# A re-ordered attention and gated-MLP kernel: K copied whole, batch 1's output turned by DMA, the flag read in mid-stream, the last two output tiles apart

## The chip, the cores and the metric

The kernel runs on one core of a Trainium2 chip. The core has five engines that work through their own queues in order and meet by semaphores: TensorE (PE; its weight loads are shown apart as PEld), VectorE (DVE), ScalarE (ACT), GpSimd (POOL) and SyncE (SP). POOL and SP also issue DMAs. The metric is the device time of one execution in microseconds; the time before is the median of three runs, 164.16 us (163.69 to 164.3).

## What is computed

Shapes: 4 batches, 8 heads, 768 positions, head width 64, 8 blocks of 96 positions.

```python
P = sort_net                                  # [B, H, 8, 8]
for _ in range(5):                            # exp, rows to sum 1, columns to sum 1
    P = exp(P - max(P)); P = P / sum(P, -1); P = P / sum(P, -2)
k_s, v_s = P mixed into the blocks of k, v    # einsum 'bhij,bhjcd->bhicd'
attn = softmax(q_block @ k_s_block.T / 8)     # within each block
x = (attn @ v_s) with heads side by side      # [B, 768, 512]
h = relu(x @ w_in); u, v = halves of h        # 512 columns each
v_n = (v - mean(v)) / sqrt(var(v) + 1e-6)
v_s = w_spatial @ v_n + b_spatial             # over the positions
out = (u * v_s) @ w_out                       # [B, 768, 512]
```

## The kernel before

The whole work is cut into small units, and the string ORDER (lines 18 to 48) lists them by hand: each item is a unit's name and its arguments, and the unit's instructions are put into the queues of their engines in this order. There is no scheduler behind it: an engine takes its own instructions in the order of the list, and waits are added where a tile is written, read or used again. PSUM has four tiles of two banks, ps0 to ps3; most units name the one that they write, so a unit also waits until the last reader of that tile is done. Letters A, D and P name the engine that copies a result out (ACT, DVE, POOL).

The units, with their lines (b a batch, hp a pair of heads, ih a half of the blocks):

- S0 loads sort_net; SK:n (line 223) is one round of the normalisation: an exp on ACT, then sums, reciprocals and products on DVE. MA (204) and MC (210) make a mask sum and a spread identity on DVE.
- L:x:b (156) issues a load on POOL's queue; BI (187) loads the bias b_bc on SP's queue. The input tiles come from a pool of 8, so later loads wait for the units that read the first ones. Each of the 8 semaphores of a queue is used in turn, so a DMA also waits for the one eight before it.
- DM (216) is six dummy matmuls on PE. PR, P0, PC, PD make the mixing matrices (PD on POOL, two parts a batch).
- QT and QQ (312, 318) turn q on PE, for one pair of heads and for two. KT (361, copies at 292 to 297) mixes and turns k. With two letters (DA, AD) its result is copied in two halves by two engines.
- VT and VB (batch 0), VM and VC (batches 1 to 3) bring the mixed v into block order; VC (400) does it by eight DMAs on SP's queue, four in each item.
- SC (413) is the scores of a pair of heads and a half, with the exp on ACT (427); AT (459) is attention times v, with a reciprocal and a product on DVE (475, 476) into x_sb.
- x_sb must be turned into xT. XT (491) does it on PE, eight transposes of 96 columns and one copy; XD (482) does a whole half by one DMA transpose on SP's queue (486). In the kernel before, batches 0 and 1 use XT, batches 2 and 3 XD.
- VP (507) and UP (549) are the two halves of x @ w_in with relu; ST, LN, LA (525 to 547) are the normalisation of v; WT (501) turns w_spatial; SP (564; a unit, not the engine of that name) is the spatial product with the bias added on DVE (575); GT (581) is the gate's product, on DVE or POOL; OP (588), OE (602) and OS (608) are the product with w_out, its copy from PSUM and its store on SP's queue.
- CK (617), CF (632) and LF (638): two checks on the sums make one flag, which every engine loads into a register; if it is set, a slower general path runs behind the main one.

The main path ends in this order:

```python
SP:3:3:0 GT:P:3:2 SP:0:3:1 OP:2:2:4 GT:D:3:1 OS:2:0 OS:2:2 OE:A:2:4 GT:D:3:0 SP:3:3:3 OP:1:3:0:0:3 GT:D:3:3
OP:0:3:4:0:3 OP:-1:3:0:3:4 OE:A:3:0:1:2 OP:3:3:2:0:3 CK OS:2:4 OP:-1:3:2:3:4 OE:D:3:2:1:2 OE:A:3:0:0:1 OP:-1:3:4:3:4
OS:3:0:1:2 OS:3:0:0:1 OE:A:3:2:0:1 OS:3:2:0:1 OS:3:2:1:2 OE:A:3:4:0:1 OS:3:4:0:1 OE:A:3:4:1:2 OS:3:4:1:2 CF:2 LF
```

OP:1:3:0:0:3 is the first three of four row blocks of tiles 0 and 1 of batch 3 in ps1, OP:-1:3:0:3:4 the fourth, which needs the last gate product. OE and OS then work on one tile of the pair.

Of the kernel before, what the change touches and what calls it, by code (L numbers as in the profile page):

```python
# [8 lines left out]
FP32 = mybir.dt.float32  # L9
# [39 lines left out]


# [12 lines left out]
def kernel(  # L63
# [19 lines left out]
    BH = B * H  # L83
    DM = H * D
# [3 lines left out]
    FC = DH // 128  # L88
# [9 lines left out]
    moe = ctx.enter_context(tc.tile_pool(name="moe", bufs=2))  # L98
# [3 lines left out]
    def ps_tile(n, dt=FP32):  # L102
        return psum.tile([128, 2, 512 if dt == FP32 else 1024], dt, name=f"ps{n}", tag=f"ps{n}")

    def copy(eng, out, in_):
        if eng == "A":
            nc.scalar.copy(out=out, in_=in_)  # L107
        else:
            nc.vector.tensor_copy(out=out, in_=in_)
# [29 lines left out]
    w_out_sb = const.tile([128, FC, DM], BF16, name="w_out_sb")  # L139
# [8 lines left out]
    st = {}  # L148
# [465 lines left out]

    def u_CK():
        nc.vector.memset(bad, 0.0)
        over = lambda col, rows, in_, op, bound, test: (
            nc.vector.tensor_reduce(out=ends[0:rows, col:col + 1], in_=in_, axis=AX.X, op=op),  # L620
            nc.vector.tensor_scalar(
                out=bad[0:rows, col:col + 1], in0=ends[0:rows, col:col + 1],
                scalar1=bound, scalar2=None, op0=test),
        )
# [103 lines left out]
```

## Time and profile before

| | |
|---|---|
| time, median of 3 runs | 164.16 us (163.69 to 164.3) |
| the profiled execution's own time | 163.99 us |
| its span, from the first instruction to the last | 162.2 us |
| PE busy | 147.9 us, 91% |
| DVE, ACT, POOL busy | 117.7, 84.3, 33.7 us |
| DMA | 23.2 MB, mean 143 GB/s |
| granted TensorE clock, mean | 0.988 |

The profile shows one execution. Busy is the time in which an engine has an instruction in work; PE's matmuls overlap, so that its busy time says only where it does not stand still. The chain of waits follows back from the last instruction what each step waited for; PE has 78% of it here, ACT 7%, DVE 6%. The costliest group is the spatial product (line 569, 192 matmuls, 33.2 us). DMA landings are counted from the issue to the last byte's semaphore.

### The profile page before, as it was taken

How to read it: one execution, taken by the hardware profiler on the slowest of the kernel's cores; microseconds unless marked ns; L12 is line 12 of the kernel's file. 1: busy time of each engine (PE TensorE's matmuls, PEld its weight loads, DVE VectorE, ACT ScalarE, POOL GpSimd, SP SyncE). 2: the span in 40 equal slices, each digit the busy share in tenths (PEclk: the TensorE clock that was granted, in tenths of full speed). 3: DMA queues.
4: the chain of work that ended last, by engine and by line, in shares of the span. 5: the costliest groups of instructions: out<-in, count | busy, mean ns of one | idle time of the engine just before them, and what ended most of it. 6: DMA issues, size and time to landing. Idle time of an engine off the chain costs nothing.

```text
span 162.2 us, 3967 instructions
## 1 busy us (share of the span) xinstructions
PE 147.9 (91%) x1646; PEld 89.5 (55%) x1657; DVE 117.7 (73%) x265; ACT 84.3 (52%) x118; POOL 33.7 (21%) x39
## 2 busy tenths in 40 slices
PE   6988999899999979999999999999999999999700
PEld 2345777756677755455657656555666445655300
DVE  4797899667897853748898888789787798267500
ACT  3144999858976476577654453557400155402420
POOL 7946322470000434280000001600000000120000
PEclk9999999999999999999999999999999999999995
DMA  2999999999999990479985996002059200243370
GB/s 12 191 204 205 203 205 205 210 220 237 271 206 204 206 172 0 69 133 148 184 188 94 225 149 195 0 36 97 0 107 237 113 0 0 91 172 129 129 250 25
DMA packets 27351, 23.20 MB, mean 143 GB/s; under 512 B 7232, under 2 KB 24128, under 8 KB 27328
## 3 DMA queue, kind: packets, MB, share of 16 engines
q0 software_dynamic: 14864, 12.19, 48.5%
q1 hardware_dynamic: 12464, 10.70, 25.8%
q8 instruction: 14, 0.23, 0.5%
q14 instruction: 9, 0.07, 0.1%
HBM read 24.78 MB, written 6.29 MB: 192 GB/s over the span
## 4 chain that ended last, share of the span: by engine, by line
PE 78%; ACT 7%; DVE 6%; DMA 2%; issue 2%; DVEq 0%; ACTq 0%
PE ps L569 20%; PE ps L557 13%; PE ps L514 13%; PE ps L595 11%; PE ps L468 4%; PE ps L422 4%; PE ps L363 3%; PE ps L390 3%; PE ps L307 3%; ACT ex L427 2%; ACT kt L107 2%; PE ps L498 2%; DMA out_dram<-o_sb 1%; PE ps L504 1%; ACT o_sb L107 1%
## 5 line engine op out<-in xcount | busy, mean ns | idle before, releaser
L569 PE MATMUL ps<-wspT,v_sb 128*128 128x384 bf16 x192 | 33.2, 326 | 0.0
L427 ACT ACTIVATE ex<-ps 96x768 bf16<-96x768 f32 x32 | 24.4, 806 | 12.4 <-PE ps L422 12.3
L585 POOL TENSOR_TENSOR gt<-z,u_sb 128x768 bf16<-128x768 f32 x7 | 11.4, 1640 | 92.7 <-DVE z L575 42.1
L569 PEld LDWEIGHTS <-v_sb 128*128 128x128 bf16 x192 | 18.2, 98 | 11.9 <-issue 0.2
L575 DVE TENSOR_TENSOR z<-ps,b_bc 128x768 f32<-128x768 f32 x16 | 15.3, 957 | 11.6 <-PE ps L569 11.5
L557 PE MATMUL ps<-xT,w_in_sb 128*128 128x384 bf16 x128 | 23.3, 326 | 0.0
L476 DVE TENSOR_TENSOR x_sb<-ps,rec_all 96x512 bf16<-96x512 f32 x32 | 22.0, 687 | 1.1
L514 PE MATMUL ps<-w_in_sb,xT 128*128 128x512 bf16 x89 | 22.2, 379 | 0.4
L595 PE MATMUL ps<-w_out_sb,gt 128*128 128x512 bf16 x93 | 22.0, 379 | 0.2
L107 ACT COPY o_sb<-ps 128x1024 f32<-128x1024 f32 (+1 forms) x12 | 9.8, 835 | 14.8 <-PE ps L595 12.9
L531 DVE BATCH_NORM_STATS2 stats<-v_sb 128x6 f32<-128x512 bf16 x24 | 16.2, 677 | 1.0 <-ACT v_sb L113 0.9
L113 ACT ACTIVATE v_sb<-ps 128x1024 bf16<-128x1024 f32 (+1 forms) x8 | 7.4, 920 | 17.6 <-PE ps L514 17.6
L557 PEld LDWEIGHTS <-w_in_sb 128*128 128x128 bf16 x128 | 11.8, 98 | 7.6
L595 PEld LDWEIGHTS <-gt 128*128 128x128 bf16 x96 | 9.2, 98 | 10.2
L514 PEld LDWEIGHTS <-xT 128*128 128x128 bf16 x96 | 9.0, 98 | 9.6 <-DVE x_sb L476 0.2
L113 ACT ACTIVATE u_sb<-ps 128x768 bf16<-128x768 f32 x13 | 10.6, 812 | 5.1 <-PE ps L557 5.0
L107 ACT CAST kt<-ps 128x768 bf16<-128x768 f32 (+1 forms) x14 | 8.7, 641 | 7.9 <-PE ps L363 5.5
L468 PEld LDWEIGHTS <-ex 96*128 96x128 bf16 x256 | 10.5, 97 | 3.6 <-issue 0.3
L468 PE MATMUL ps<-vb,ex 96*128 96x65 bf16 x256 | 11.9, 193 | 0.1
L219 PE MATMUL ps<-warm 128*128 128x512 bf16 x35 | 9.9, 436 | 1.3 <-DVE warm L192 1.3
L422 PE MATMUL ps<-qT,kt 64*128 64x96 bf16 x256 | 9.5, 204 | 1.6 <-ACT kt L107 1.3
L422 PEld LDWEIGHTS <-kt 64*128 64x128 bf16 x256 | 6.2, 94 | 6.9 <-issue 3.8
(87 smaller groups left out, 179.0 us busy)
## 6 DMA issues: line engine op xcount, KB each, us to landing
out_dram<-o_sb SPq DMA_DIRECT2D x9, 512.0 KB, 4.3
q_in<-in_q_dram POOLq DMA_DIRECT2D x4, 768.0 KB, 18.0
k_in<-in_k_dram POOLq DMA_DIRECT2D x4, 768.0 KB, 15.1
v_in<-in_v_dram POOLq DMA_DIRECT2D x4, 768.0 KB, 21.5
vb<-vm SPq DMA_DIRECT2D x24, 99.0 KB, 3.1
out_dram<-o_sb SPq DMA_DIRECT2D x6, 256.0 KB, 3.2
ws_in<-in_moe_w_spatial_dram POOLq DMA_DIRECT2D x2, 576.0 KB, 26.4
w_in_sb<-in_moe_w_in_dram POOLq DMA_DIRECT2D x2, 512.0 KB, 26.0
```

The costliest lines, as they stand in the source:

```text
L107: nc.scalar.copy(out=out, in_=in_)
L113: nc.scalar.activation(out=out, in_=in_, func=AF.Relu)
L422: nc.tensor.matmul(t[:, hh, 0:HW].rearrange("p (g x) -> p g x", g=G)[:, :, ii * TB:(ii + 1) * TB], lhsT=kT[rows, i * BLK:i * BLK + 128], r ...
L427: nc.scalar.activation(out=e_tile(b, hp, ih).rearrange("p h (x g) -> p h x g", g=G), in_=t[0:BLK, :, 0:HW].rearrange("p h (g x) -> p h x g ...
L468: nc.tensor.matmul(t[:, hh, ii * VW:ii * VW + D + 1], lhsT=e[:, c:c + 128], rhs=vb[b % 2][:, ih * NI + ii, 2 * hp + hh, 0:D + 1], start=Tr ...
L476: nc.vector.tensor_mul(out=x_sb[:, hp].rearrange("p i (h d) -> p h i d", h=2), in0=tv[:, :, :, 0:D], in1=_raw_ap(rec, 0, [rec.ap[0], [NI, ...
L514: nc.tensor.matmul(t[:, x, :], lhsT=st["xT", b][:, n // 3, kc, (n % 3) * 128:(n % 3 + 1) * 128], rhs=w_in_sb[:, kc, DH:DFF], start=(kc == ...
L531: nc.vector.bn_stats(out=stats, in_=st["v_sb", b, n])
L557: nc.tensor.matmul(t[:, x, 0:HW], lhsT=w_in_sb[:, kc, mc * 128:(mc + 1) * 128], rhs=st["xT", b][:, ih, kc, :], start=(kc == 0), stop=(kc = ...
L569: nc.tensor.matmul(t[:, x, 0:HW], lhsT=st["v_sb", b, n][:, mc * 128:(mc + 1) * 128], rhs=wspT[:, 3 * x:3 * x + 3, n, :], start=(n == 0), s ...
L575: nc.vector.tensor_add(out=z.rearrange("p (x c) -> p x c", x=2), in0=t[:, :, 0:HW], in1=b_bc.rearrange("p (x c) -> p x c", x=2),)
L595: nc.tensor.matmul(t[:, x, :], lhsT=st["gt", b, mc][:, (n0 + x) * 128:(n0 + x + 1) * 128], rhs=w_out_sb[:, mc, :], start=(mc == 0), stop=( ...
```

## The change

ORDER is written anew, and three units are added for the last two output tiles. What differs in it:

- Every KT copies its result whole, by one engine (eight on ACT, eight on DVE). Before, seven of 16 were copied in two halves.
- Batch 1's x is turned by two DMA transposes (XD:1:0, XD:1:1) instead of four XT units; batch 0 keeps its four XT.
- BI, the load of the bias, stands at the start instead of in batch 1's scores. The loads come in another order: q of batch 1 ahead of v and k, v of batch 2 ahead of its q and k, w_out behind k of batch 3, and q of batch 3 earlier.
- The order of heads, halves and units and the engine of many copies differ: five of the six W copies are on DVE instead of three, ten of the 16 gate products on POOL instead of seven, two of the 13 relus of VP less on DVE.
- CK and CF stand ahead of the last six SP units and LF ahead of the last four; before, LF stood behind the last store. The branch stays at the end.
- Tiles 4 and 5 of batch 3 are computed, copied and stored one by one (OH, OI, OJ), in PSUM tiles and output tiles of their own; the output tiles come from the pool of z.
- All six DM units are there in both.

```diff
--- before.py
+++ after.py
@@ -16,35 +16,35 @@
 
 
 ORDER = """
-S0 CO SK:0 L:q:0:0:8 L:k:0:0:8 L:v:0:0:8 L:v:1:0:8 BH SK:1 SK:2 L:k:1:0:8 ID IV:2 MC IV:0 DM:1:6:512 L:q:1:0:8 SK:3
-L:wv MA DM:3:6:512 DM:1:6:512 DM:2:6:512 SK:4 L:wsb QT:1:A:0:0 MB QT:0:D:0:1 QT:3:A:0:2 DM:2:6:512 PR:3 DM:2:6:512
-P0:0:2 KT:1:A:0:0 P0:6:8 L:wu P0:4:6 PC:D P0:2:4 PD:1:0:4 QT:0:D:0:3 L:wsa IV:1 PD:1:4:8 KT:2:DA:0:1 KT:3:DA:0:3
-SC:1:0:0:0 SC:0:0:1:1 KT:2:D:0:2 SC:3:0:0:1 L:q:2:0:8 VT:1:D:0:0 SC:0:0:2:0 L:k:2:0:8 VT:2:D:0:1 SC:3:0:3:1 VB:1:D:0:0
-VT:0:A:0:2 VB:2:D:0:1 VT:3:A:0:3 AT:1:0:0:1 VB:0:A:0:2 L:v:2:0:8 AT:2:0:0:0 L:wo VB:3:D:0:3 PD:3:0:4 SC:1:0:3:0
-AT:0:0:1:1 SC:2:0:1:0 SC:3:0:2:1 AT:1:0:3:1 VM:2:A:1:0 AT:0:0:1:0 VM:3:A:1:1 AT:1:0:2:1 VM:2:A:1:2 XT:0:D:0:1:0
-KT:3:A:1:2 AT:1:0:2:0 KT:0:A:1:0 AT:2:0:3:0 XT:3:A:0:1:2 KT:0:A:1:3 QQ:1:D:1:0 VM:2:A:1:3 XT:0:D:0:0:2 XT:3:D:0:0:0
-SC:1:1:0:0 QQ:2:D:1:2 VC:1:0:4 KT:0:A:1:1 VP:1:D:0:0:1 SC:3:1:2:1 ST:0:0 SC:0:1:3:1 VP:2:A:0:4:5 WT:3:A:5 WT:1:D:4
-VP:0:A:0:3 ST:0:5 PD:2:0:4 SC:2:1:1:0 ST:0:3 SC:1:1:2:0 UP:3:A:0:1:0 VP:2:A:0:2 VC:1:4:8 ST:0:1 ST:0:4 AT:0:1:0:0
-ST:0:2 WT:1:A:3 SC:3:1:3:0 LN:0:0:6 UP:2:A:0:0:1 AT:0:1:2:0 AT:1:1:3:0 LA:0:0 PD:2:4:8 UP:3:A:0:1:1 WT:0:D:0 LA:0:2
-LA:0:1 LA:0:4 AT:2:1:2:1 LA:0:3 XT:1:A:1:0:2 LA:0:5 L:v:3:0:8 WT:3:A:1 UP:0:A:0:0:0 WT:3:D:2 BI SC:1:1:0:1 QQ:2:A:2:2
-AT:3:1:1:0 AT:0:1:3:1 SP:1:0:3 SC:2:1:1:1 XT:0:D:1:1:2 XT:3:A:1:0:0 AT:1:1:0:1 AT:2:1:1:1 SP:0:0:2 XT:2:A:1:1:0
-GT:P:0:3 KT:1:AD:2:3 KT:3:AD:2:2 KT:0:DA:2:0 KT:2:A:2:1 GT:P:0:2 QQ:1:A:2:0 SC:0:2:3:0 VM:3:D:2:3 SP:2:0:1 VM:1:A:2:2
-VM:0:A:2:1 VP:3:D:1:0:1 VM:2:A:2:0 SP:1:0:0 SC:0:2:2:1 SC:2:2:1:1 GT:P:0:1 VC:2:4:8 VC:2:0:4 ST:1:1 VP:3:A:1:4:5
-SC:1:2:1:0 SC:0:2:3:1 GT:P:0:0 UP:2:A:1:0:0 PD:3:4:8 ST:1:0 ST:1:4 VP:3:D:1:2:3 VM:2:A:3:3 VM:1:A:3:0 OP:0:0:2 ST:1:2
-OE:A:0:2 L:k:3:0:8 AT:1:2:3:1 VM:2:A:3:2 UP:3:A:1:1:0 ST:1:5 AT:0:2:2:1 ST:1:3 VM:2:D:3:1 L:q:3:0:8 UP:1:A:1:0:1
-AT:3:2:1:1 LN:1:0:6 UP:0:A:1:1:1 LA:1:1 AT:1:2:3:0 OP:2:0:0 LA:1:0 SC:1:2:0:1 SC:0:2:2:0 OP:3:0:4 LA:1:5 OS:0:2
-OE:D:0:0 LA:1:3 LA:1:4 LA:1:2 AT:2:2:0:1 AT:0:2:2:0 SP:1:1:0 OE:A:0:4 XD:2:1 SC:2:2:0:0 KT:0:DA:3:2 QQ:3:D:3:2
-KT:1:D:3:1 KT:2:AD:3:0 SP:0:1:2 KT:2:A:3:3 OS:0:4 GT:D:1:0 QQ:1:A:3:0 AT:3:2:1:0 AT:0:2:0:0 VP:2:D:2:4:5 VC:3:0:4
-VC:3:4:8 SC:3:3:3:0 SC:1:3:3:1 ST:2:4 XD:2:0 SP:0:1:1 SC:2:3:2:1 GT:D:1:2 SC:1:3:1:1 SP:3:1:3 AT:0:3:3:0 GT:P:1:3
-AT:2:3:3:1 VP:1:A:2:2:3 ST:2:5 VP:0:A:2:0:1 OS:0:0 AT:1:3:2:1 GT:P:1:1 ST:2:3 UP:2:D:2:0:1 OP:1:1:2 SC:3:3:0:0
-OE:D:1:2 ST:2:2 SC:2:3:1:0 UP:0:A:2:1:0 SC:1:3:0:1 ST:2:1 ST:2:0 LN:2:0:6 SC:3:3:2:0 UP:2:D:2:0:0 AT:0:3:1:1 LA:2:5
-LA:2:4 LA:2:2 OS:1:2 UP:1:A:2:1:1 OP:2:1:0 AT:1:3:0:0 OE:A:1:0 LA:2:0 LA:2:3 LA:2:1 OP:3:1:4 AT:2:3:1:0 AT:0:3:2:0
-SP:1:2:1 XD:3:0 AT:2:3:0:1 XD:3:1 GT:D:2:1 OE:A:1:4 SP:0:2:0 SP:1:2:3 GT:D:2:0 SP:0:2:2 OS:1:4 UP:3:D:3:0:0 OS:1:0
-VP:0:D:3:2:3 GT:D:2:2 VP:1:A:3:0:1 ST:3:3 GT:D:2:3 ST:3:2 UP:3:A:3:0:1 VP:0:A:3:4:5 ST:3:1 OP:3:2:2 ST:3:0 OP:2:2:0
-ST:3:5 ST:3:4 OE:A:2:2 LN:3:0:6 UP:1:A:3:1:1 LA:3:1 UP:0:A:3:1:0 LA:3:5 LA:3:3 LA:3:0 LA:3:2 OE:A:2:0 LA:3:4 SP:1:3:2
-SP:3:3:0 GT:P:3:2 SP:0:3:1 OP:2:2:4 GT:D:3:1 OS:2:0 OS:2:2 OE:A:2:4 GT:D:3:0 SP:3:3:3 OP:1:3:0:0:3 GT:D:3:3
-OP:0:3:4:0:3 OP:-1:3:0:3:4 OE:A:3:0:1:2 OP:3:3:2:0:3 CK OS:2:4 OP:-1:3:2:3:4 OE:D:3:2:1:2 OE:A:3:0:0:1 OP:-1:3:4:3:4
-OS:3:0:1:2 OS:3:0:0:1 OE:A:3:2:0:1 OS:3:2:0:1 OS:3:2:1:2 OE:A:3:4:0:1 OS:3:4:0:1 OE:A:3:4:1:2 OS:3:4:1:2 CF:2 LF
+S0 CO BI L:q:0:0:8 DM:0:6:512 DM:2:6:512 BH L:k:0:0:8 IV:1 SK:0 L:v:0:0:8 ID L:q:1:0:8 SK:1 SK:2 DM:1:6:512 L:v:1:0:8
+MA L:k:1:0:8 L:wv MC IV:2 SK:3 DM:2:6:512 L:wsb L:wu SK:4 QT:1:A:0:1 QT:3:A:0:0 MB QT:0:D:0:3 DM:2:6:512 QT:1:A:0:2
+PR:3 IV:0 P0:0:2 P0:2:4 DM:2:6:512 P0:6:8 P0:4:6 PC:A L:wsa PD:1:0:4 PD:1:4:8 KT:1:A:0:0 L:v:2:0:8 KT:0:D:0:2
+KT:2:A:0:3 KT:3:D:0:1 SC:1:0:0:1 SC:0:0:0:0 SC:1:0:3:1 VT:3:D:0:0 SC:0:0:2:0 VT:2:A:0:1 VB:3:D:0:0 VT:1:A:0:2
+L:q:2:0:8 VB:2:D:0:1 AT:0:0:0:1 SC:3:0:3:0 VT:1:A:0:3 L:k:2:0:8 PD:2:4:8 QQ:2:D:1:2 SC:0:0:1:0 AT:3:0:0:0 VB:1:D:0:2
+VB:2:A:0:3 QQ:0:D:1:0 SC:3:0:2:1 PD:2:0:4 AT:1:0:3:1 SC:2:0:1:1 AT:0:0:1:0 VM:3:A:1:1 AT:1:0:2:1 VM:2:A:1:3 AT:0:0:2:0
+VM:3:A:1:2 AT:1:0:3:0 L:v:3:0:8 XT:2:A:0:1:2 VM:3:A:1:0 L:k:3:0:8 KT:0:D:1:1 XT:1:A:0:0:2 XT:2:D:0:0:0 KT:3:A:1:3
+KT:0:A:1:2 KT:1:D:1:0 AT:2:0:1:1 VP:3:A:0:0:1 PD:3:4:8 XT:2:D:0:1:0 VP:1:A:0:2 ST:0:1 L:wo WT:2:D:5 SC:0:1:2:0
+VC:1:0:4 ST:0:2 ST:0:0 SC:3:1:0:0 VP:1:A:0:3 ST:0:3 VP:0:D:0:4:5 PD:3:0:4 SC:1:1:1:0 ST:0:4 SC:2:1:3:0 ST:0:5
+UP:3:A:0:0:0 LN:0:0:6 AT:1:1:0:0 VC:1:4:8 LA:0:2 LA:0:1 UP:0:A:0:0:1 LA:0:3 SC:3:1:0:1 WT:2:A:1 AT:1:1:2:0 LA:0:0
+LA:0:4 L:q:3:0:8 UP:0:A:0:1:0 AT:3:1:3:0 AT:1:1:1:0 LA:0:5 UP:2:A:0:1:1 WT:3:D:3 VM:0:A:2:3 AT:1:1:0:1 SC:2:1:2:1
+XD:1:0 WT:3:D:4 WT:0:D:0 SC:1:1:3:1 WT:2:D:2 VM:3:A:2:2 AT:0:1:2:1 VM:1:D:2:0 VM:2:D:2:1 SC:3:1:1:1 SP:0:0:2
+AT:2:1:3:1 GT:P:0:2 AT:1:1:1:1 SP:3:0:1 SP:0:0:0 KT:3:A:2:3 KT:2:A:2:1 QQ:1:D:2:0 KT:0:D:2:2 QQ:3:A:2:2 KT:2:D:2:0
+VP:1:D:1:0:1 GT:P:0:1 VC:2:4:8 ST:1:1 GT:D:0:0 SC:0:2:3:1 SC:3:2:0:0 SP:2:0:3 SC:0:2:2:1 XD:1:1 SC:1:2:0:1
+UP:3:A:1:0:1 VC:2:0:4 AT:0:2:3:1 VP:2:D:1:2:3 SC:0:2:1:1 SC:1:2:3:0 VP:3:A:1:4:5 AT:2:2:2:1 AT:1:2:0:0 UP:0:A:1:0:0
+ST:1:5 VM:3:A:3:3 AT:2:2:1:1 KT:1:A:3:3 ST:1:3 UP:0:A:1:1:1 SC:3:2:1:0 SC:1:2:2:0 GT:P:0:3 ST:1:4 OP:2:0:2 ST:1:0
+ST:1:2 OE:A:0:2 VM:3:A:3:2 AT:1:2:0:1 OP:0:0:0 AT:3:2:3:0 AT:2:2:2:0 LN:1:0:6 OS:0:2 LA:1:0 OP:1:0:4 OE:A:0:0
+VM:0:A:3:1 UP:2:A:1:1:0 VM:0:A:3:0 XD:2:1 OE:D:0:4 LA:1:1 VC:3:0:4 AT:1:2:1:0 UP:3:D:2:0:1 KT:2:A:3:1 LA:1:5
+QQ:0:D:3:2 LA:1:3 QQ:1:A:3:0 KT:3:D:3:2 LA:1:4 KT:2:A:3:0 OS:0:0 VP:0:A:2:4:5 SC:3:3:0:0 LA:1:2 SC:1:3:2:0 SP:2:1:2
+AT:0:3:0:0 XD:2:0 SP:3:1:3 SC:2:3:1:1 GT:P:1:2 SC:0:3:3:1 SP:1:1:1 GT:P:1:3 AT:3:3:2:0 SP:0:1:0 SC:3:3:1:0 SC:2:3:3:0
+VC:3:4:8 GT:D:1:1 VP:1:A:2:2:3 AT:3:3:1:0 UP:2:A:2:0:0 AT:0:3:3:0 VP:1:A:2:0:1 ST:2:5 GT:P:1:0 ST:2:3 AT:0:3:1:1
+OP:2:1:4 ST:2:0 SC:1:3:0:1 OE:D:1:4 SC:3:3:2:1 OP:0:1:0 XD:3:0 ST:2:4 ST:2:2 OS:0:4 OE:A:1:0 AT:2:3:0:1 ST:2:1
+UP:3:A:2:1:0 LN:2:0:6 UP:0:A:3:1:0 OS:1:4 AT:2:3:3:1 AT:1:3:2:1 UP:3:A:2:1:1 OS:1:0 LA:2:0 LA:2:2 XD:3:1 VP:0:A:3:0:1
+LA:2:1 LA:2:4 LA:2:3 LA:2:5 OP:1:1:2 SP:3:2:0 OE:A:1:2 VP:2:A:3:4:5 CK ST:3:0 ST:3:1 VP:1:A:3:2:3 ST:3:3 GT:D:2:0
+SP:3:2:3 ST:3:4 UP:0:A:3:1:1 UP:2:A:3:0:0 ST:3:2 ST:3:5 OS:1:2 LN:3:0:6 CF:1 LA:3:3 LA:3:2 GT:P:2:3 LA:3:5 LA:3:0
+SP:3:2:2 LA:3:1 LA:3:4 GT:P:2:2 UP:1:A:3:0:1 SP:0:2:1 GT:D:2:1 LF SP:3:3:0 OP:1:2:2 SP:2:3:2 GT:P:3:0 OE:D:2:2
+SP:3:3:1 OP:0:2:4 GT:P:3:2 OE:A:2:4 OP:3:2:0 GT:D:3:1 OS:2:2 SP:0:3:3 OP:2:3:0:0:3 OE:A:2:0 OP:0:3:2:0:3 GT:D:3:3
+OP:-1:3:0:3:4 OS:2:4 OH:1:3:5:0:3 OE:A:3:0:0:1 OP:-1:3:2:3:4 OS:2:0 OS:3:0:0:1 OE:D:3:0:1:2 OH:-1:3:5:3:4 OS:3:0:1:2
+OE:D:3:2:1:2 OH:3:3:4:0:3 OE:A:3:2:0:1 OI:D:3:5 OS:3:2:1:2 OH:-1:3:4:3:4 OI:A:3:4 OJ:3:5 OJ:3:4 OS:3:2:0:1
 """
 
 
@@ -613,6 +613,25 @@
         )
 
 
+
+    def u_OH(ps, b, n, lo=0, hi=4):
+        b, n, lo, hi = int(b), int(n), int(lo), int(hi)
+        if lo == 0:
+            st["o1_ps", b, n] = ps_tile(ps)
+        for mc in range(lo, hi):
+            nc.tensor.matmul(
+                st["o1_ps", b, n][:, 0, :], lhsT=st["gt", b, mc][:, n * 128:(n + 1) * 128], rhs=w_out_sb[:, mc, :],
+                start=(mc == 0), stop=(mc == FC - 1),
+            )
+
+    def u_OI(eng, b, n):
+        b, n = int(b), int(n)
+        st["o1", b, n] = moe.tile([128, S], FP32, name="o1_sb", tag="z", bufs=2)
+        copy(eng, st["o1", b, n][:, 0:DM], st["o1_ps", b, n][:, 0, :])
+
+    def u_OJ(b, n):
+        b, n = int(b), int(n)
+        nc.sync.dma_start(out=out[b, n * 128:(n + 1) * 128, :], in_=st["o1", b, n][:, 0:DM])
 
     def u_CK():
         nc.vector.memset(bad, 0.0)
```

## The prediction

> **What bounds the kernel now.** I read the busy table by stage first, cut where the order of the work changes: the end of the normalisation chain (11.48 us), the first VP unit (32.84), the first SP unit (49.83), the end of the K copies of batch 2 (66), the end of the last SP unit (147.8). Columns: PE, weight loads, DVE, ACT and POOL busy (instructions), granted clock, DMA share, GB/s.
>
> ```profile
> 11.48:32.84 21.36, 19.58 (x427) 15.29 (x427) 17.54 (x36) 16.85 (x23) 7.68 (x9) 1.00 1.29 205
> 32.84:49.83 16.99, 16.89 (x222) 11.01 (x221) 13.52 (x32) 13.94 (x21) 3.04 (x3) 1.00 1.23 232
> 49.83:66.00 16.17, 15.24 (x194) 10.12 (x192) 10.36 (x17) 9.73 (x13) 4.92 (x3) 1.00 0.83 131
> 66.00:138.11 72.11, 71.73 (x672) 41.08 (x676) 59.46 (x114) 34.39 (x46) 7.69 (x6) 1.00 0.56 111
> 147.80:162.20 14.40, 5.27 (x25) 2.22 (x23) 4.39 (x16) 2.73 (x5) 0.00 (x0) 0.86 0.42 150
> ```
>
> From 32.84 to 147.8 PE is idle for only 1.5 us and keeps its full clock: it is the bound, and what is taken off it counts unless a new wait takes its place. Before that the copies on ACT and DVE and the loads pace it; after 147.8 it is the way from matmul to store.
>
> The chain of waits shows where PE does wait: 55.97 to 59.23 has hardly a matmul in it.
>
> ```profile
> 55.97 0.80 ACT xT L107
> 56.76 0.39 ACT kt L107
> 57.18 0.42 DVE kt L109
> ...
> 58.12 0.56 DVE kt L109
> 58.70 0.49 ACT kt L107
> 59.23 0.34 PE ps L422 x8
> ```
>
> The two halves of one K copy run one behind the other, on two engines: 0.56 + 0.49 and the handover, 1.07 us. A whole copy takes 0.80 on ACT (row: 800 ns, x7) and 0.95 on DVE (952 ns, x2).
>
> Then the DMA transposes and the flag reads (minimum/median/maximum ns), and stores and loads where they overlap.
>
> ```profile
> L486 SPq DMA_TRANSPOSE xT<-x_sb x4: 1435/1462/1551, 85.9 to 120.3; - x4
> DMA to landing us min/median/max: 4.6/5.1/5.5
> ```
>
> ```profile
> L639 PEldq TENSOR_LOAD <-flag x1: 490/490/490, 153.6 to 153.6; - x1
> L639 SPq TENSOR_LOAD <-flag x1: 912/912/912, 156.2 to 156.2; - x1
> ```
>
> ```profile
> out_dram<-o_sb SPq DMA_DIRECT2D x1, 512.0 KB, 8.2
> ```
>
> The last line is the first output store, issued at 76.0 beside the loads of batch 3. The same store alone lands in 2.8 us (140.05 to 142.87). The last loads end at 85.2, so all four transposes of before (85.9 and later) ran without loads beside them.
>
> **PE's work, step by step.** Unit lengths are those of the chain: SP (12 matmuls) 1.95, UP 1.30, VP 0.865 a tile, OP 1.74, SC 0.25, AT 0.24, VM 0.325, KT 0.42, QQ 0.70, XT 0.40, WT 0.335.
>
> The head. All loads of q, k and v go through POOL's queue, which is saturated from 4 to 46 us (slices of about 205 GB/s); its first six land at 8.75, 12.58, 16.41, 21.06, 24.90 and 28.74. The new order loads q of batch 1 fourth and k sixth, so the first K unit of batch 1 (KT:0:D:1:1) can't start before 28.8; before, its k came fifth and it ran at 26.46. What the head changes otherwise lies under this: the mask sum L204 now stands beside the spread copy L210 behind the third round and no longer under the fourth round's exp (+0.43 on the chain), one QT moves ahead of PR, and the walk through the copies (a kt copy every 0.70 on ACT, 0.88 on DVE; an AT's reciprocal and multiply every 0.84) reaches the same place at about 28.6. Dummies: 6 units of 6 in both, none gained.
>
> From 28.8 on PE still has, up to the end of the last SP unit: 16 SP 31.2, 16 UP 20.8, 24 VP tiles 20.8, 9 OP 15.6, 24 SC 6.0, 25 AT 6.0, 8 VM 2.6, 12 KT 5.0, 4 QQ 2.8, 3 XT 1.2, 6 WT 2.0, the flag matmul 0.1: **114.1**, so 142.9 without a wait. The same sum for before, from 26.46, is 117.6 (four XT of batch 1, 1.6 us, are in it, and two QQ, one VM and one AT more), and it took 121.3: 3.7 of waits.
>
> Waits of the changed kernel, walking the in-order queues with these rows:
> - 0.9 up to SP:2:0:3 in AT and copy handovers (AT, WT and ST all on DVE: five W copies instead of three). Bounds 0 to 2.
> - K copies whole: no wait. In batch 2, KT, KT, QQ, KT, QQ, KT keep PE busy for 2.9 us while each copy is done 0.8 to 0.95 after its unit. The 0.9 of idle there goes; late next is k of batch 2, which I put at 55 (third behind the last weights) against 56.5.
> - XD:1:0 is issued at about 46.2, when the last AT of its half is through DVE, and is needed at 59.4 by VP. XD:1:1 is issued at 54.8 and needed at 64.1 by UP:3:A:1:0:1, 9.3 later. The loads of v3, k3, wo and q3 keep the queue full until about 70, so both run beside loads, which no run shows. Below: 5.1, the row without loads (no wait). Above: the store's ratio, 8.2/2.8 times 5.1, 15. Nearest is the store on the same queue, of like size (512 against 384 KB): it loses 5.4 us, and so do the vb copies (2.7 to 7.1 and more). I take 5.1 + 5.4 = 10.5: XD:1:0 lands at 56.7 and is hidden; XD:1:1 at 65.3, **1.2 of wait**. Queued behind it on SP are four vb copies (0.6 each); their AT is 5 us later.
> - XD:2:1 now stands behind store OS:0:2 in SP's queue and is needed 5 us later: 0.2. XD:3:1 the same, 0.5 (bounds 0 and 2 together).
> - Flag early: PE loads it in mid-stream. 0 (its sequencer runs ahead) to 0.6 (0.49 and the gap); I take 0.4. The other engines' loads (0.48 to 0.91) fall where they idle. At the end nothing is gained: SP's load lay at 156.19 to 157.10, under the last store's landing (159.77).
> - CF waits for DVE's checks, and LA of batch 3 stand just ahead of SP:3:3:0: 0.3.
>
> Sum 3.5: the last SP unit ends at **146.4** instead of 147.8.
>
> On the transposes the Trainium skill ("DMA: Bandwidth & Descriptors", Queues, rings and completion order) says that a DMA engine takes the queues that have work in turn, packet by packet. By that a transpose beside one loading queue would only have its moving part doubled, which would hide XD:1:1 and make the sum 159.8, rival 1 below; the rows beside loads speak for more.
>
> **The tail**, from the end of the last SP unit (T). Before, the last store is issued at 155.79 = T + 7.99: ACT waits for DVE's half of tile pair 2, then for the store that holds the o buffer, then copies tile 4 and 5 by itself (0.59 each). After: 24 matmuls of 0.217 end at T + 5.2 as before; ACT copies tile 0 at T + 3.1, DVE tiles 1, 3 and 5 from T + 3.75 (0.69 each, so to T + 5.9), ACT tile 2 from 5.2 and tile 4 to 6.4, both last ones in z buffers that are free. SP issues six stores 0.46 apart at the closest: the last, OS:3:2:0:1 behind both OJ, at T + 6.9. It lands 4.0 later and ends 2.4 after that, as before. **-1.1** (bounds 0 and -1.6).
>
> Moving b_bc to the start puts 393 KB beside the first loads. Between 30 and 46 us hardware queues moved 1.20 MB and POOL's queue 0.75 MB less than at 204 GB/s; at this ratio b_bc costs 0.25 MB, 1.2 us. I take 0: POOL's first bytes move at about 4 us, and a store of 512 KB issued at 1.2 would have landed by then. Bounds 0 and 1.2.
>
> **Sum.** 1.4 + 1.1 = 2.5. The profiled run took 163.99 (span 162.2 and 1.8 around it), so 161.5; the median of the three runs lies 0.17 higher: **161.7**.
>
> **Rivals.**
> 1. *The transposes are hidden* (for it: PE's distance of 9.3 is near twice the 5.1; against: 8.2 for a plain store). The three XD waits, 1.9, go: 159.8.
> 2. *A port or the early b_bc takes half the gain.* GT:P:2:2 starts on POOL just when the last two LA of batch 3 run on DVE, and SP:3:3:0 waits for them with 0.3 to spare. In before no POOL GT (1.64 us each) stood beside an LA, so whether one holds up the other isn't shown; if LA waits out a GT, 1.64 - 0.3 = 1.3 is lost: 163.0. b_bc's 1.2 alone gives 162.9, and both together 164.2. I count the case, 163.6 in its middle, as no change. The Trainium skill ("SBUF — State Buffer", Who interferes with whom) states such a lock between VectorE's two-port modes and GpSimd, held for a whole instruction; no row here tests it.
> 3. *Slower: the loads starve the transposes.* If XD:1:1 grows by the store's ratio to 15, it lands at 69.8, and UP waits 5.7 instead of 1.2: 161.7 + 4.5 = 166.2. It turns from gain to loss where XD:1:1 takes over 13 us. For it: vb copies of 99 KB, 2.7 alone, took up to 8.2 beside loads. Against: those grew by a fixed 5, not by a factor.
>
> **Chances.** Forecast 0.46, rival 1 0.12, rival 2 0.17, rival 3 0.25. A measurement of this kernel tells about 0.5% (0.8 us) from no change: faster 0.58, same 0.17, slower 0.25. The range goes from a little below rival 1 to rival 3: 159.4 to 166.0.
>
> **What would show it.** Right: no kt copies of 384 columns; no PE gap like that of 55.97; XD:1:1 landing 9 to 12 us from issue and an UP that waits 1 to 2 us; the last SP unit ending at 146 to 147; the last store issued under 7.2 after it. Wrong: k of batch 1 landing after 29.5 (b_bc), an XD over 13 us, POOL GT or LA stretched near the last SP units, PE idle for over 1 us between 33 and 53.

## The result, and the profile after

The changed kernel takes **172.95 us** (median of four runs, 171.99 to 177.54; the last figure is of a disturbed run, and the ratios here and below leave such runs out) against 164.23 for the kernel before beside it: a ratio of 1.0523, 95% interval 1.0486 to 1.0559. It is 5.2% slower. The forecast was 161.7 us, with a range of 159.4 to 166.0: number, range and sign were wrong. The profiled execution took 171.99 us, its span 169.9.

The busy table of the changed kernel, cut at the first VP unit (32.75), the first SP unit (51.86), the end of the K copies of batch 2 (62.70), around a gap, and at the end of the last SP unit (158.29); columns as in the table of before:

```profile
32.75:51.86 19.11, 18.47 (x225) 11.47 (x222) 17.54 (x41) 13.75 (x20) 4.85 (x5) 1.00 1.24 220
51.86:62.70 10.84, 10.32 (x153) 7.13 (x154) 8.74 (x12) 3.75 (x4) 3.27 (x2) 1.00 1.30 189
...
66.50:74.25 7.75, 0.04 (x2) 0.00 (x1) 1.01 (x2) 1.48 (x2) 1.64 (x1) 0.74 1.29 178
74.25:82.00 7.75, 7.75 (x67) 4.11 (x68) 2.46 (x5) 2.94 (x4) 0.00 (x0) 0.82 0.44 85
...
158.29:169.94 11.65, 5.18 (x24) 2.16 (x22) 3.80 (x5) 1.66 (x3) 0.00 (x0) 0.82 0.49 184
```

One row stands out: for 7.75 us PE does nothing, nor does any other engine for long, while the DMA engines are full (1.29). In the row behind it PE is busy throughout, but at a granted clock of 0.82. The timeline of PE shows where:

```profile
66.03 0.51 PE L422 MATMUL ps<-qT,kt 64*128 64x96 bf16 x16
74.25 2.74 PE L557 MATMUL ps<-xT,w_in_sb 128*128 128x384 bf16 x8 [7.71 <-DMA xT<-x_sb]
```

This is UP:3:A:1:0:1, the first unit that needs half 1 of batch 1's xT. It waits for XD:1:1, and then takes 2.74 us for eight matmuls that take 1.46 elsewhere (122.34). The transposes of the changed kernel, durations of the issuing instruction (ns) and time from issue to landing:

```profile
L486 SPq DMA_TRANSPOSE xT<-x_sb x6: 1441/2182/7233, 47.8 to 125.9; - x6
...
DMA to landing us min/median/max: 3.7/5.0/17.5
```

XD:1:0 is issued at 47.76 and lands at 61.65 (13.9 us); XD:1:1 at 56.68 and lands at 74.20 (17.5 us). The four of batches 2 and 3, with no loads beside them, take 3.7 to 5.6. All waits of PE from 30 us on:

```profile
PE ps L557 <- DMA xT<-x_sb: 7.7, 1, 7.7
PE ps L557 <- ACT o_sb L107: 1.2, 1, 1.2
PE ps L595 <- DVE gt L585: 0.7, 1, 0.7
PE ps L504 <- DMA ws_in<-in_moe_w_spatial_dram: 0.6, 1, 0.6
PE ps L514 <- DVE kt L109: 0.5, 1, 0.5
```

The loss is all ahead of 158.29: the last SP unit ends 10.5 us later than in before, and from there to the end of the span it is 11.65 us instead of 14.40.

### The profile page after: what moved, and what is told of

It is laid out like the page before. It is cut to its first block, busy times and chain, and to the rows that moved or that the text cites. A ratio compares the mean times of both kernels' runs of the same rounds, so it can differ in the third digit from the quotient of the medians.

```text
span 169.9 us, 3905 instructions
## 1 busy us (share of the span) xinstructions
PE 148.5 (87%) x1625; PEld 87.7 (52%) x1625; DVE 114.0 (67%) x257; ACT 82.2 (48%) x112; POOL 39.7 (23%) x42
## 4 chain that ended last, share of the span: by engine, by line
PE 48%; DMA 37%; DVE 6%; ACT 2%; issue 2%; POOL 1%; SPq 0%; ACTq 0%; POOLq 0%
DMA ws_in<-in_moe_w_spatial_dram 17%; PE ps L569 12%; DMA xT<-x_sb 10%; PE ps L595 9%; PE ps L557 9%; PE ps L514 8%; DMA k_in<-in_k_dram 7%; PE ps L468 3%; DMA out_dram<-o_sb 3%; PE ps L422 2%; DVE z L575 2%; PE ps L390 2%; DVE stats L531 1%; DVE v_sb L543 1%; PE ps L504 1%
## 5 line engine op out<-in xcount | busy, mean ns | idle before, releaser
L585 POOL TENSOR_TENSOR gt<-z,u_sb 128x768 bf16<-128x768 f32 x10 | 17.1, 1707 | 95.9 <-DVE rec_all L475 49.0
L557 PE MATMUL ps<-xT,w_in_sb 128*128 128x384 bf16 x128 | 24.6, 338 | 8.9 <-DMA xT<-x_sb 7.7
L595 PE MATMUL ps<-w_out_sb,gt 128*128 128x512 bf16 x88 | 20.8, 379 | 0.7 <-DVE gt L585 0.7
L113 ACT ACTIVATE u_sb<-ps 128x768 bf16<-128x768 f32 x15 | 12.2, 810 | 18.3 <-PE ps L557 17.8
L107 ACT COPY o_sb<-ps 128x1024 f32<-128x1024 f32 (+1 forms) x9 | 7.7, 871 | 20.5 <-PE ps L595 16.8
L475 DVE RECIPROCAL rec_all<-ps 96x8 f32<-96x8 f32 x32 | 6.2, 194 | 16.5 <-PE ps L468 16.5
L595 PEld LDWEIGHTS <-gt 128*128 128x128 bf16 x88 | 8.2, 98 | 10.1 <-DVE gt L585 1.2
L113 ACT ACTIVATE v_sb<-ps 128x1024 bf16<-128x1024 f32 (+1 forms) x10 | 9.4, 938 | 8.1 <-PE ps L514 8.1
L107 ACT CAST kt<-ps 128x768 bf16<-128x768 f32 x9 | 6.9, 803 | 7.0 <-PE ps L363 7.0
L543 DVE TENSOR_SCALAR v_sb<-v_sb,mv,rstd 128x512 bf16<-128x512 bf16 x24 | 9.9, 458 | 0.4 <-ACT rstd L538 0.4
```

Source lines behind the costliest of these rows:

```text
L113: nc.scalar.activation(out=out, in_=in_, func=AF.Relu)
L557: nc.tensor.matmul(t[:, x, 0:HW], lhsT=w_in_sb[:, kc, mc * 128:(mc + 1) * 128], rhs=st["xT", b][:, ih, kc, :], start=(kc == 0), stop=(kc = ...
L585: eng.tensor_mul(out=gt, in0=st["z", b, mc], in1=st["u", b, mc // 2][:, mc % 2])
L595: nc.tensor.matmul(t[:, x, :], lhsT=st["gt", b, mc][:, (n0 + x) * 128:(n0 + x + 1) * 128], rhs=w_out_sb[:, mc, :], start=(mc == 0), stop=( ...
```

## The experiments

**Theory**: the packets of batch 1's transposes and those of POOL's loads, which are in flight until 78, hold each other up; the early b_bc adds its own transfer time to every load. **Rivals**: the new order loses by itself and the wait only shows where it ends; the copies ahead of XD:1:1 in SP's queue are the cause; b_bc is hidden. Times are medians, ratios are to the kernel before on the same chip with 95% intervals. In the edits, `...` stands for units left out.

**1. Batch 1 turned on PE.** In the changed kernel:

```diff
-XD:1:0 ... XD:1:1
+XT:2:A:1:0:0 XT:1:A:1:0:2 SP:0:0:0 XT:2:A:1:1:0 ... XT:0:A:1:1:2 VP:1:D:1:0:1
```

> The changed kernel with batch 1's two DMA transposes replaced by four XT units on PE (1.6 us of PE work). Theory (loads starve the transposes): the 7.7 us wait of UP:3:A:1:0:1 and about 1.2 us of slower clock behind it go, 1.6 come: 172.9 - 8.9 + 1.6 = 165 to 166, and the vb copies of batch 2 land 8 us or less after issue. Rival (the new order itself loses, the wait only moves to k of batch 3, w_out or q of batch 3, which land at 70 to 78): PE waits there instead, 169 or more.

Measured: 164.79 us, ratio 1.0039 (1.0014 to 1.0065), a little under the theory's 165 to 166. 8.0 us of the loss are gone with this one part (172.79, the median of the changed kernel's other three runs, less 164.79), and from 30 us on no wait over 0.7 appears. The rival that the order itself loses falls.

**2. Transposes kept, loads behind.**

```diff
-L:v:3:0:8 ... L:k:3:0:8 ... L:wo ... L:q:3:0:8
+GT:P:0:1 L:v:3:0:8 L:k:3:0:8 L:wo L:q:3:0:8
```

> The changed kernel with both DMA transposes kept; the loads of v3, k3, w_out and q3 are issued behind the gate product GT:P:0:1 on POOL, so that XD:1:1 has at most k of batch 2 beside it. Theory (loads starve the transposes): XD:1:1 lands 5 to 7 us after issue, no wait over 1 us at UP:3:A:1:0:1, 164 to 166, with a small wait for v or k of batch 3 possible. Rival (two transposes and eight vb copies on one queue are slow by themselves): XD:1:1 still takes over 12 us, PE waits over 3 us, 168 or more.

Measured: ratio 0.9962 (0.9933 to 0.9990); the ten runs that it counts have a mean of 163.4, the median of all twelve is 164.09. XD:1:1, issued at 56.58 (56.68 in the changed kernel) but with the loads only issued from 59 on, lands at 61.09: 4.5 us instead of 17.5. XD:1:0 had k of batch 2 beside it and took 10.0. PE's waits from 30 us on:

```profile
PE ps L557 <- ACT o_sb L107: 1.2, 1, 1.2
PE ps L595 <- DVE gt L585: 0.7, 1, 0.7
PE ps L390 <- DMA v_in<-in_v_dram: 0.2, 1, 0.2
```

So it is the loads, not the transposes themselves. The runs lie in two groups, 162.4 to 162.5 and 164.1 to 164.3, with one between. The lower group was granted 0.986 to 0.996 of the TensorE clock, the upper 0.976 to 0.979; the trace is of the lower. A stretch of half clock like the one in experiment 3 would fit the 1.7 us, but no trace of the upper group shows it, and why there are two stays open.

**3. As 1, with b_bc late.**

```diff
-S0 CO BI L:q:0:0:8
+S0 CO L:q:0:0:8 ... VC:1:4:8 BI LA:0:2
```

> As the kernel with batch 1 turned on PE, and the load of b_bc back behind the first batch's vb copies (issued near 38 us). Theory (the early b_bc delays the whole chain of loads by 1.2 us): q of batch 0 lands at 8.75 instead of 9.97, k of batch 1 at 28.8 instead of 30.05, and the time is 1.0 to 1.2 lower than that of its partner. Rival (it is taken up by slack, or comes back at the W loads that land behind it): within 0.4 of its partner.

Measured: 163.19 us, 0.9939 (0.9922 to 0.9957): 1.6 less than its partner, more than the theory's 1.0 to 1.2. The issue lines of the first load, us to landing, first in the changed kernel, then here:

```profile
q_in<-in_q_dram POOLq DMA_DIRECT2D x1, 768.0 KB, 8.7
b_bc<-in_moe_b_spatial_dram SPq DMA_DIRECT2D x1, 384.0 KB, 4.1
```

```profile
q_in<-in_q_dram POOLq DMA_DIRECT2D x1, 768.0 KB, 7.4
```

k of batch 1 lands at 30.05 in the one (29.93 in the partner) and 28.57 in the other: what b_bc takes at the start is still there at the sixth load. It does not stay to the end: v of batch 2 lands at 47.42 in the partner and 46.98 here, because here b_bc is moved in between (issued at 35.83, landed at 44.87).

Nor is the 1.6 this delay alone. In the partner's profiled run PE waits 2.3 us for the first q, and then has half its clock for 3.4 us, which is 1.7 us of clock lost. First the partner, then this run:

```profile
10.78:14.20 3.42, 3.42 (x30) 1.55 (x24) 1.48 (x6) 1.49 (x2) 0.68 (x2) 0.50 1.32 204
```

```profile
10.78:14.20 3.42, 3.42 (x48) 1.80 (x48) 2.82 (x10) 1.69 (x3) 0.74 (x1) 1.00 1.32 204
```

The partner's three runs with a mean clock over 0.99 took 163.91 to 164.38, only 0.7 to 1.2 more than 163.19. So the early b_bc costs time, and how much of it is the loads' delay and how much the clock is not separated.

**4. XD:1:1 ahead of the vb copies.**

```diff
-VC:2:4:8 ... SC:0:2:2:1 XD:1:1 SC:1:2:0:1
+AT:1:1:1:1 XD:1:1 SP:3:0:1 ... VC:2:4:8
```

> The changed kernel with XD:1:1 put ahead of SP:3:0:1 and of the vb copies of batch 2 in SP's queue, so that it is issued at about 53 instead of 56.7. Theory (loads starve it): it still takes 15 us or more, lands near 70, PE waits 3 to 5 us: 168 to 170. Rival (it is slow because four vb copies stand ahead of it on the same rings): it takes under 9 us, lands by 62, no wait: 164 to 165.

Measured: 172.13 us, 1.0487 (1.0456 to 1.0519). My issue time was wrong: x of half 1 is only through DVE at 57.06, and XD:1:1 was issued at 57.08. It took 15.4 us with no vb copy between it and XD:1:0, so the copies alone are not the cause:

```profile
72.56 2.74 PE L557 MATMUL ps<-xT,w_in_sb 128*128 128x384 bf16 x8 [5.93 <-DMA xT<-x_sb]
```

The wait is 1.8 shorter than in the changed kernel, the time only 0.7 (172.13 against 172.79). Most of the difference is the clock: behind the gap it stays at 0.50 for 5.6 us here, 2.8 us lost, and for 2.8 us (74.25 to 77.07) in the changed kernel, 1.4 lost.

```profile
72.56:78.19 5.63, 5.56 (x22) 2.58 (x23) 0.89 (x2) 0.81 (x1) 0.00 (x0) 0.50 1.10 227
```

**5. Half 0 on PE, half 1 by DMA, loads as in the changed kernel.** 

```diff
-XD:1:0
+SP:3:0:1 XT:2:A:1:0:0 XT:1:A:1:0:2 SP:0:0:0
```

> The changed kernel, all loads where they are, with half 0 of batch 1 turned by two XT units on PE and only half 1 by DMA. Theory (packets in turn, and the second transpose stood behind the first): XD:1:1 now has the queue for itself but for four vb copies, 1,570 packets at the 5.3 ns that a pair of packets took beside the loads, 8.3 us and 3 to 5 to start, landing at 68 to 70; PE waits 1 to 3 us, 166.5 to 169. Rival (each transpose is slow by itself beside loads, whatever stands ahead): 15 us or more, landing at 72 or later, 170 to 173.

Measured: 168.99 us, 1.0301 (1.0266 to 1.0336). The time fits the theory, the landing (73.0, 15.2 us after issue) and the wait (5.1) the rival. Both were half right. The four vb copies ahead land at 63.10, and XD:1:1 needs 9.9 us from there; in the changed kernel the copies land at 64.44 and it needs 9.8. One transpose beside the loads takes some 10 us once its queue is free, not the 8.3 that I put down (1,570 packets at the pace of 52 to 57 us, 944 pairs in 5 us), and what stands ahead in the queue comes on top. XD:1:0 of the changed kernel, with nothing ahead of it, agrees in another way: in the first 4.0 us after its issue (47.76 to 51.80) SP's queue moved only 4 packets, and it landed 9.85 us after that. Part of what the 8.3 lacks is a stop of all queues of some 0.7 us in each of the two (58.9 to 59.6 and 67.4 to 68.1, at 9 to 53 GB/s); its cause stays open. The profiled run of this kernel, at 170.93, also waited 2.0 us for its first q and then had half its clock for 3.4 us; the other four took 168.97 to 169.57.

What the engines move in that time, in the changed kernel from 61.7 to 73 us (queue, kind: packets, MB, share of 16 engines):

```profile
q0 software_dynamic: 1783, 1.47, 86.5%
q1 hardware_dynamic: 1784, 0.66, 40.9%
```

q0 is POOL's queue of loads, q1 SP's. Here they move **one packet for one**, with hardly a packet's difference (in experiment 5 itself, from 63.1 to 73, it is 1,501 and 1,600), and a transpose's packets are small: from 57.42 to 61.09 experiment 2 moved 1,602 under 512 B, about one transpose. So it is the number of its packets, not its 384 KB, that sets how long it lies beside a load; no run varies the size of the packets, so this rests on the counts. The Trainium skill ("DMA: Bandwidth & Descriptors", Queues, rings and completion order) states this turn by packets, and the trace agrees: 1,783 and 1,784. The counts do not show whether a turn is one of the profile's packets or several.

**6. Only the two transposes, in the kernel before.**

```diff
-XT:1:A:1:0:2 ... XT:0:D:1:1:2 XT:3:A:1:0:0 ... XT:2:A:1:1:0
+AT:3:1:1:0 XD:1:0 ... AT:2:1:1:1 XD:1:1 SP:0:0:2
```

> The kernel before with only batch 1's four XT units replaced by two DMA transposes, issued near 50.5 and 54.5; its loads end at 61.2. Theory (packets of a transpose and of the loads are moved in turn, one for one, and the second transpose waits for the first in its queue): the first takes 11 to 13 us, the second lands at 66 to 71, PE waits 1 to 6 us, the 1.6 us of XT come off: 164 to 169. Rival (each transpose takes the forecast's 10.5 us by itself): the first lands at 61, the second at 65, no wait of over 1 us, 162.5 to 163.3.

Measured: 167.84 us, 1.0243 (1.0207 to 1.0280). XD:1:0 took 13.8 us, longer than the theory's 11 to 13, and landed at 64.59, just as the last load (v of batch 3) did, at 64.39; XD:1:1, with no load left beside it, followed at 65.88. PE waits 2.8 us for the two, and 1.4 more for DVE and ACT at places where before it did not. This part of the change loses by itself, in the old order too:

```profile
64.63 1.90 PE L514 MATMUL ps<-w_in_sb,xT 128*128 128x512 bf16 x7 [2.45 <-DMA xT<-x_sb]
```

**7. Only whole K copies, in the kernel before.**

```diff
-KT:1:AD:2:3 KT:3:AD:2:2 KT:0:DA:2:0 KT:2:A:2:1
+KT:1:D:2:3 KT:3:A:2:2 KT:0:D:2:0 KT:2:A:2:1
```

The other four split copies are made whole too.

> The kernel before with its seven split K copies made whole (four on DVE, three on ACT), nothing else changed. Theory of the forecast: the 0.9 us of idle at 55.97 to 59.23 goes and the rest is hidden, 0.7 to 0.9 less than before, 163.2. Rival (the idle there is the wait for k of batch 2, or the whole copies make scores wait elsewhere): within 0.4 of before, or slower.

Measured: 163.17 us, 0.9949 (0.9934 to 0.9964): 0.9 less, as forecast. The idle of 0.29 and 0.58 in front of QQ and SC is gone:

```profile
57.34 0.86 PE L307 MATMUL ps<-ident,q_in 128*64 128x128 bf16 x24
58.20 0.35 PE L422 MATMUL ps<-qT,kt 64*128 64x96 bf16 x8
```

**8. Only the end, in the kernel before** (OH, OI, OJ; CK, CF and LF last of all):

```diff
-OP:3:3:2:0:3 CK OS:2:4 ... OP:-1:3:4:3:4 ... OE:A:3:4:0:1 OS:3:4:0:1 OE:A:3:4:1:2 OS:3:4:1:2 CF:2 LF
+OH:3:3:5:0:3 ... OH:2:3:4:0:3 ... OI:D:3:5 ... OI:A:3:4 OJ:3:5 OJ:3:4 OS:3:2:0:1 CK CF:2 LF
```

> The kernel before with only the end changed: the last two output tiles computed, copied and stored one by one from buffers of their own, the flag still made and read behind the last store. Forecast's term: the last store is issued 6.9 to 7.1 after the end of the last SP unit instead of 7.99, 1.1 less than before, 163.0. Other size (the 2.6 us that the changed kernel gains from the last SP unit to the end is all of the tail): 161.5. Rival (half of that came from reading the flag early, or the tail's order does nothing by itself): 163.3 to 164.

Measured: 162.89 us, 0.9912 (0.9881 to 0.9942): 1.4 less. The last store is issued at T + 6.52 and lands at 157.6, but the span ends 3.8 later, against 1.8 in the changed kernel: now that the stores are done sooner, the flag's matmul stands behind them and waits for DVE's checks (file lines here are one higher):

```profile
PE ps L654 <- DVE bad L641: 2.2, 1, 2.2
```

**9. Both causes undone, both transposes kept**, the edits of 2 and 3:

```diff
-S0 CO BI ... L:v:3:0:8 ... L:k:3:0:8 ... L:wo ... L:q:3:0:8
+S0 CO ... VC:1:4:8 BI ... GT:P:0:1 L:v:3:0:8 L:k:3:0:8 L:wo L:q:3:0:8
```

> The changed kernel with the late loads behind GT:P:0:1 and the load of b_bc back behind the first batch's vb copies: both suspected causes undone, both DMA transposes kept. Theory (the two causes are all that the forecast missed, their costs add): the loads' 1.2 to 1.6 comes off the 163.4 of the kernel with the late loads alone, 161.8 to 162.3, close to the forecast of 161.7. Rival (b_bc now lands beside XD:1:0 or the W loads and holds those up): 163 or more.

Measured: 162.36 us, 0.9904 (0.9876 to 0.9933), 1.0 less than the mean of 2, as the theory adds them up. The traces don't show that sum: k of batch 1 lands 1.4 earlier than in 2 (28.59 against 29.97), but a wait for v of batch 3 grows from 0.2 to 0.9, the price of the late loads, and the last SP unit ends at 148.4 in both. Against the lower group of 2, at 162.4, nothing is gained. XD:1:0 takes 10.9, XD:1:1 4.7.

**10. As 9, with a store ahead.**

```diff
-OP:0:1:0 XD:3:0 ST:2:4 ST:2:2 OS:0:4 OE:A:1:0
+OP:0:1:0 OS:0:4 XD:3:0 ST:2:4 ST:2:2 OE:A:1:0
```

> As its partner (late loads behind GT:P:0:1, b_bc late), with the store OS:0:4 ahead of XD:3:0 in SP's queue. Theory (the 1.2 us wait of UP:0:A:3:1:0 for ACT is the copy OE:A:1:0, which waits for the o buffer that OS:0:4 holds): that wait goes, 1.0 to 1.2 less than the partner. Rival (PE's wait is taken over by XD:3:0, now later, or by the next copy): less than 0.4 less.

Measured: 160.76 us, 0.9816 (0.9787 to 0.9846), 1.6 less, more than the theory's 1.0 to 1.2, and the wait for ACT o_sb is gone from PE's list. In the changed kernel OS:0:4 is issued behind XD:3:0 and lands at 121.12; only then can OE:A:1:0 write into the o buffer, and the next UP needs its PSUM tile:

```profile
121.27 1.01 ACT L107 COPY o_sb<-ps 128x1024 f32<-128x1024 f32 x1 [2.10 <-PE ps L557]
```

The view puts this wait down to a matmul that ends at 121.12 too; that it was the store is what the experiment shows.

**11. As 9, with two LA ahead.**

```diff
-SP:3:2:2 LA:3:1 LA:3:4 GT:P:2:2
+LA:3:1 LA:3:4 SP:3:2:2 GT:P:2:2
```

> As its partner (late loads behind GT:P:0:1, b_bc late), with LA:3:1 and LA:3:4 ahead of SP:3:2:2, so that no LA runs while POOL has GT:P:2:2. Theory (the LA that takes 1.73 instead of 0.40 us waits for POOL's instruction to end, and this makes the 0.7 us wait of OP:1:2:2): all LA take 0.41 or less, that wait goes, 0.5 to 0.8 less than the partner. Rival (the LA is long for another reason, such as its data or its wait): one LA still takes over 1 us. Rival 2 (the lock is there, but DVE is late anyway): LA short, time within 0.3 of the partner.

Measured: 161.82 us, 0.9870 (0.9844 to 0.9895), 0.5 less, though the two intervals overlap. The trace is plainer. LA in the changed kernel, the gate product on POOL beside it, then LA here (ns, minimum/median/maximum):

```profile
L543 DVE TENSOR_SCALAR v_sb<-v_sb,mv,rstd x24: 398/403/1728, 43.1 to 143.7; 128x512 bf16<-128x512 bf16 x24
```

```profile
143.56 1.67 POOL L585 TENSOR_TENSOR gt<-z,u_sb 128x768 bf16<-128x768 f32 x1 [3.60 <-DVE z L575]
```

```profile
L543 DVE TENSOR_SCALAR v_sb<-v_sb,mv,rstd x24: 398/403/415, 42.4 to 132.8; 128x512 bf16<-128x512 bf16 x24
```

The LA that begins at 143.66 ends with POOL's product and not before. PE's wait for gt falls from 0.7 to 0.2. The Trainium skill ("SBUF — State Buffer", Who interferes with whom) states that the engine that comes second waits out the whole instruction: 1.73 instead of 0.40 agrees. The 0.5 of time is not this alone: in the same traces the wait for v of batch 3 falls from 0.9 to 0.3, which the edit does not aim at.

**12. All mends together**: 9, 10 and 11, with v of batch 3 one unit earlier:

```diff
-GT:P:0:2 ... GT:P:0:1 L:v:3:0:8 L:k:3:0:8
+GT:P:0:2 L:v:3:0:8 ... GT:P:0:1 L:k:3:0:8
```

> All mends together: the changed kernel with v3 behind GT:P:0:2, with k3, w_out and q3 behind GT:P:0:1, with b_bc late, OS:0:4 ahead of XD:3:0 and the two LA ahead of SP:3:2:2. Theory (costs add): 160.76 less 0.5 (LA) less 0 to 0.9 (wait for v of batch 3): 159.4 to 160.3. Rival (v3 beside XD:1:1 delays it, and UP waits for it instead): XD:1:1 over 7 us, 160.8 or more.

Measured: **160.42 us**, 0.9765 (0.9734 to 0.9796): 2.3% faster than before and 7% faster than the changed kernel. The time lies just above the theory's 160.3; the rival's sign came (XD:1:1 takes 7.8 us), its time did not, since nobody waits for XD:1:1. v of batch 3 is waited for 1.2, so moving it brought nothing.

## Why the prediction was wrong, point by point

Put as the forecast put it, T = 146.4 was 28.8 (k of batch 1) + 114.1 (PE's units) + 3.5 (waits). The trace has 30.05 + 117.36 (busy) + 10.9 (idle) = 158.3. Of the 11.9 between them:

- **The step that failed is XD:1:1, put at 10.5 us and 1.2 of wait; it took 17.5 and 7.7: 6.5 us.** The forecast added a store's extra 5.4 to 5.1 and counted from the issue. Two things were missing. The transposes' own part beside the loads is 9.8, but it begins when the queue is free: XD:1:0 had landed at 61.65 and the vb copies at 64.44, 7.8 us after the issue. The forecast had counted the four vb copies behind XD:1:1, not XD:1:0 and the four ahead. That its 10.5 lies near 9.8 is luck: the extra is no fixed 5.4 but a turn of packets, one for one. And "only doubled", by which rival 1 hid the wait, takes a load's packets to be as short as a transpose's, where they are 824 against 370 B on average with the vb copies among the latter. Rival 3 named the mechanism and its point, over 13 us, but went by the store's ratio to 15 and had only 0.25.
- **The slower clock behind the gap**, in no term: 0.82 over 7.75 us is 1.4, and in experiment 4 it was 2.8. The Trainium skill ("TensorE: Matmul & The Clock Gate", Part 1) states that PE's clock falls after an idle window of about 3.4 us; the gap of 7.7 and the 0.74 and 0.82 agree. In experiment 6, idle for 2.5, the clock shows no dip there; but the waits of 2.3 and 2.0 for the first q, in the profiled runs of experiments 1 and 5, were followed by half clock. So the length of one wait does not decide it alone, and what else does stays open.
- **b_bc at the start, put at 0; 1.25 us** by k of batch 1. The two pairs of runs say 1.6 and 1.0, but neither is that delay alone (experiments 3 and 9). The bound of 1.2 from the traffic between 30 and 46 us was the right row; the argument that b_bc would be done before POOL's first bytes fell: it landed at 5.35, inside the first load's time.
- **PE's units**: 117.36 less the 1.4 of slow clock is 116.0, 1.9 over the sum of unit lengths. Before shows the same, 119.40 busy against 117.6. So of its 3.7 "waits" only 1.9 was idle time.
- **Other idle time**: 3.2 us against the forecast's 2.3. Its waits for XD:2:1, XD:3:1 and the flag didn't come; 1.2 for the o buffer, 0.7 for gt (rival 2's lock, by another way than SP:3:3:0, and half its price of 1.3) and 0.6 for W did. That XD:3:0 would hold up OS:0:4 was not walked.
- **K copies whole**: right in cause and size, 0.9 (experiment 7).
- **The end**: -1.1 forecast, -2.75 in the trace. The last store is issued at T + 6.89, as said (6.9), but lands 2.98 later, not 4.0, and the span ends 1.8 after it, not 2.4. The end alone brought 1.4 (experiment 8); "nothing is gained" by the early flag was wrong, since shorter stores no longer cover it.

With the mends of experiment 12 the same sum is 28.6 + 115.5 + 2.3 = 146.4, the T of the forecast to the tenth. That is luck in part: PE's units are 1.4 over the forecast and the waits 1.2 under it, and experiments 10 and 11 mended things that the forecast had not seen.

## What to carry to other kernels

Before a DMA takes work from an engine, look at what its queue and the others hold in that stretch: count its packets, count them one for one against a load that is in flight, and start the clock when the DMAs ahead of it in its own queue have landed. The same move was free for batches 2 and 3, where no load ran, and cost 3.6 us in the kernel before (experiment 6) and 8.0 in the changed one (experiment 1). A transfer placed at the head of a saturated chain of loads delays the loads behind it: b_bc by 1.3 to 1.5 us, from the first load to the sixth.

## What the runs showed of the hardware that was not expected

- The issue of a transpose itself can be long: 1.44 us with free queues, 3.42 and 7.23 beside the loads. Everything behind it on SP's queue waits as long.
- Between two queues that both held work, packets were moved one for one (719 and 719 from 57 to 61.7; 1,783 and 1,784 from 61.7 to 73), whatever their size.
- An LA of 0.40 us waited out a POOL gate product of 1.67; and a POOL product that began during one on DVE took 2.28 instead of 1.64. The bias addition (0.96), which reads PSUM, kept its time beside them.
- One wait of 7.7 us cost 1.4 more in clock afterwards, one of 5.9 (experiment 4) 2.8, one of 2.5 (experiment 6) nothing; what a stall takes can be more than its length.
